# An engine order left to the scheduler, four tiles for spilled sums, and the start of MLP 2, in an attention kernel with two MLPs

## The chip, the core and the metric

The kernel runs on one core of a Trainium2 chip. The metric is the device time of one execution, in microseconds (us). The core has five engines, each with a queue of its own that it works off in order: TensorE (PE; matmuls, weight loads as PEld), VectorE (DVE), ScalarE (ACT), GpSimd (POOL) and SyncE (SP), which issues all transfers (DMAs) here. An instruction waits until what it needs is there, and everything behind it on its engine waits with it. Results of matmuls stand in PSUM, of which the program uses eight banks (four of each of two tags, a and b); the other memory on the core is SBUF.

## The reference, cut to what matters

Attention of 8 heads (4 batches, 512 local positions with a window of 32 to each side, 32 global ones), then an MLP with a gate (MLP 1), then an MLP with a rational function (MLP 2), on 2176 tokens of 512 numbers.

```python
def _moe_ref(x, w_gate, w_val, w_out):            # 512 -> 1536 -> 512
    g = x @ w_gate
    silu = g * (1.0 / (1.0 + np.exp(-g)))
    val = x @ w_val
    return (silu * val @ w_out).astype(np.float32)

def _moe2_ref(x, w_in, w_out, a, b):              # 512 -> 2048 -> 512
    h = x @ w_in
    h2 = h * h
    h3 = h2 * h
    P = a[0] + a[1] * h + a[2] * h2 + a[3] * h3
    Q = 1.0 + np.abs(b[0]) * np.abs(h) + np.abs(b[1]) * h2
    g = P / (Q + 1e-06)
    return (g @ w_out).astype(np.float32)

def reference(**kwargs):
    attn_out = _attn_ref(**attn_kwargs)
    B, H, S, D = attn_out.shape
    x = np.ascontiguousarray(attn_out.transpose(0, 2, 1, 3)).reshape(B * S, H * D)
    x = _moe_ref(x=x, **moe_kwargs)
    return _moe2_ref(x=x, **moe2_kwargs)
```

## The kernel before

Every matmul of the MLPs is done in three: both operands are split into a high part (a cast, ScalarE or VectorE, L126 or L128) and a low part (a subtraction, GpSimd or VectorE, L129), and `mm3` (L485 to L487) adds high x high, high x low and low x high. The weights come as 64-bit floats; each block of 512 columns is loaded as 32-bit halves into one of two tiles `stage` (L134) and converted by GpSimd (L144), ScalarE (L146) and VectorE (L147, L149).

The first part (to about 277 us) is the attention with a third of MLP 1's hidden layer woven in. Its partial sums of MLP 1 go to a tensor `yas` in HBM.

The second part is the rest of MLP 1. It runs in eight passes `v`: batch `v % 4`, first with hidden blocks 4 to 7 (v = 0 to 3), then with blocks 8 to 11 (v = 4 to 7). A pass has four units `u`, one for each hidden block. A unit makes gate and value by a scheme with seven products of half blocks in place of eight: seven `prod` of six matmuls each, into the PSUM banks X and Z (tag b) and Y (tag a). Three copies on ScalarE take intermediate sums out of PSUM: L769 (of X), L773 (of Z) and L776 (of X again, before TensorE adds the last product to X). Between L773 and L776 stands the Silu (L754) of the unit before, which waits for an addition of VectorE (L753). TensorE goes on with X after L776, so a late L776 holds TensorE. The operands of these products are x and differences of its halves (`x_prep`, parts 0 to 7: differences on VectorE, L721, high parts on ScalarE, low parts on VectorE).

The products with the output weights of a pass are made in the next pass, in eight *pieces* (`piece`), two or three to a unit (in v = 1 four in units 1 and 2). For v < 4, VectorE adds a piece to the partial sum fetched from `yas` (L806) into one of two tiles "y" (L814), and it is stored back (L815). For v = 4 to 7, a whole block is fetched into `x32` (L822), and the pieces are added there (L818): that is MLP 2's input. Meanwhile MLP 2's weights are converted, one block in units 0 and 1 and two in units 2 and 3, and stored in a tensor `w2s` (L860). In the last pass they are fetched back (L871) and split (`w2_item`).

The third part is MLP 2, in tiles of 384 tokens by one of 16 hidden blocks: `p2_mm`, then ScalarE (L1038 to L1040, L1067, L1068, L1073) and VectorE (L1047 to L1059), then the low part (L1062, on GpSimd for the first four tiles) and `p2_out` (L1086 to L1088), four tiles behind.

The order of TensorE and SyncE is that in which the code is written, everywhere. For VectorE, ScalarE and GpSimd a scheduler sets the order when the kernel is built, by a cost model of its own, except inside `tc.manual_schedule()`: there it is the written order too. The kernel before enters this ahead of the second part (`ordered[0].__enter__()`) and leaves it ahead of `p2_mm(0)`.

Of the kernel before, what the change touches and what calls it, by code (L numbers as in the profile page):

```python
# [77 lines left out]
def tile_attn_moe_moe(  # L78
# [575 lines left out]
    for name, n, count in (("ab", HT, 2), ("v2", HT, 2), ("s", 2 * HT, 2), ("t", 2 * HT, 3), ("y", HT, 2),  # L654
                           ("e", 256, 1), ("st", 512, 2)):
        FA[name] = [("f", at_ + n * i, n) for i in range(count)]
        at_ += n * count
# [55 lines left out]
    def x_prep(v, part):  # L713
        b = v % B
        t0 = b * S
        b11, b12 = x32[:, 0:2, t0:t0 + HT], x32[:, 0:2, t0 + HT:t0 + S]
        b21, b22 = x32[:, 2:4, t0:t0 + HT], x32[:, 2:4, t0 + HT:t0 + S]

        def diff(which, p, q):
            t = tv[v, which] = take["t"]().rearrange("p (k c) -> p k c", k=2)  # L720
            nc.vector.tensor_tensor(out=t, in0=p, in1=q, op=ALU.subtract)  # L721
            return t
        if part == 0:
            x_split(v, B11, b11)
        elif part == 1:
            x_split(v, T1, diff(T1, b12, b11))
        elif part == 2:
            x_split(v, T2, diff(T2, b22, tv[v, T1]))
        elif part == 3:
            diff(T4, b21, tv[v, T2])  # L730
            diff(T3, b22, b12)
        elif part == 4:
            x_split(v, B21, b21)
        elif part == 5:
            x_split(v, T3, tv[v, T3])
        elif part == 6:
            x_split(v, B22, b22)
        else:
            x_split(v, T4, tv[v, T4])
# [68 lines left out]
    def piece_evac(v, i):  # L808
# [3 lines left out]
        if v < B:  # L812
            y = py.pop((v, i))
            nc.vector.tensor_tensor(out=y, in0=o, in1=y, op=ALU.add)  # L814
            nc.sync.dma_start(yas[:, j, t0:t0 + HT], y)  # L815
        else:
            x = x32[:, j, t0:t0 + HT]
            nc.vector.tensor_tensor(out=x, in0=o, in1=x, op=ALU.add)  # L818

# [77 lines left out]
    ordered = [tc.manual_schedule()]  # L897
    ordered[0].__enter__()
# [27 lines left out]
    first_pieces = {1: (0, 4), 2: (4, 8)}  # L926
    for v in range(NV):
        fs = FB[v // B]
        for u, f in enumerate(fs):
# [16 lines left out]
            def before():  # L946
                todo(words[0])
                if (v, u) == (4, 2):
                    todo("")
# [6 lines left out]
            def after():  # L956
                n0, n1 = (first_pieces if v == 1 else pieces_of).get(u, (0, 0)) if v else (0, 0)
                if v and v - 1 < B:
                    for i in range(n0, min(n0 + 2, n1)):
                        piece_load(v - 1, i)  # L960
# [3 lines left out]
                for i in range(n0, n1):  # L964
                    piece(v - 1, i, FB[(v - 1) // B], True, True)
                    if v - 1 < B and i + 2 < n1:
                        piece_load(v - 1, i + 2)
# [11 lines left out]
                if v >= B and u == 0:  # L979
# [13 lines left out]
    for k in range(KD):  # L993
        split_y(0, k)
    for i in range(4):
        piece(v, i, fs[:3], True, False)
    for i in range(4):
        piece(v, i, fs[3:], False, True)
    for i in range(4, 8):
        piece(v, i, fs, True, True)  # L1000
    w2_item(24, nc.vector, nc.gpsimd)

    total = NC2 * F2
    ph, pt, pq, pr, pg = {}, {}, {}, {}, {}

    def width(n):
        c = n // F2
        return cols2[c][1] - cols2[c][0]

    def p2_mm(n):  # L1010
        c, f = divmod(n, F2)
        w = width(n)
        h = psum("b")
        for k in range(KD):
            mm3(h[:, :w], wt2[f, 0], slice(128 * k, 128 * k + 128), xs[("y", c), k], slice(0, w),
                k == 0, k == KD - 1)
        ph[n] = h[:, :w]

    warm_act = const.tile([128, 1], F32, name="warm_act")
    nc.scalar.activation(warm_act, cqt, AF.Abs_reciprocal_sqrt)  # L1020
    ordered.pop().__exit__(None, None, None)
    p2_mm(0)
    p2_mm(1)

# [79 lines left out]
    for n in range(total + 4):  # L1104
# [21 lines left out]
        if n < 8:  # L1126
            w2_item(24 + n + 1, nc.vector, nc.gpsimd)
# [62 lines left out]
```

## Time and profile before

| what | us |
|---|---|
| median of 3 runs (lowest, highest) | 1080.92 (1076.33, 1082.48) |
| the profiled execution, its own time | 1079.84 |
| its span, first to last instruction | 1078.1 |
| TensorE busy | 944.5 (88%) |
| VectorE busy | 775.4 (72%) |
| ScalarE busy | 620.5 (58%) |
| GpSimd busy | 228.7 (21%) |

The mean granted clock of TensorE is 0.935 of full speed. Busy times are sums over the whole span, and a busy TensorE may be one at half its clock. "Idle before" is the time that an engine stood still ahead of an instruction, with the instruction or transfer that ended it. A wait for several things is put down to the last.

### The profile page before, as it was taken

To read this page: it belongs to the slowest core of one execution; us is meant where nothing else is said; L and a number is where in the kernel's file an instruction comes from. 1 tells how busy PE (TensorE), PEld (TensorE's weight loads), DVE (VectorE), ACT (ScalarE), POOL (GpSimd) and SP (SyncE) were. 2 spreads that over 40 slices of the span, in tenths; PEclk is the share of its full clock that TensorE was granted. 3 is DMA by queue.
4 is the path that set the end of the run, shared out by engine and by line. 5 is a ranking of instruction groups with operands and counts; after the bars stand their busy time and mean duration, and the time that the engine had idled before them with its cause. 6 is when DMAs were issued, how large, how long until landed. Compare 5 with 4: busy or idle time off the path is not lost.

```text
span 1078.1 us, 20901 instructions
## 1 busy us (share of the span) xinstructions
PE 944.5 (88%) x7986; PEld 865.5 (80%) x7988; DVE 775.4 (72%) x1740; ACT 620.5 (58%) x1450; POOL 228.7 (21%) x233
## 2 busy tenths in 40 slices
PE   6989999999676787767678999779999999999998
PEld 4778888889676677666677999669999999999996
DVE  5876667667354555465567755999888988888897
ACT  5755566544353233334244343557877878878786
POOL 2420000002433222335142235840000000000012
PEclk8889999999778888978789999889999999999999
DMA  9846878634113344435353332310100101001010
GB/s 341 294 143 232 279 226 277 194 116 126 61 40 113 130 140 135 146 112 200 115 186 124 105 130 79 118 40 1 30 1 1 30 1 30 1 1 30 1 30 21
DMA packets 62981, 118.02 MB, mean 109 GB/s; under 512 B 8352, under 2 KB 31904, under 8 KB 62880
## 3 DMA queue, kind: packets, MB, share of 16 engines
q1 hardware_dynamic: 62880, 116.68, 32.7%
q8 instruction: 63, 1.03, 0.4%
q14 instruction: 38, 0.31, 0.1%
HBM read 88.61 MB, written 28.05 MB: 108 GB/s over the span
## 4 chain that ended last, share of the span: by engine, by line
PE 42%; DMA 20%; DVE 15%; issue 10%; POOL 6%; ACT 5%; SPq 1%; POOLq 0%; DVEq 0%; ACTq 0%
PE b L485 7%; PE b L487 7%; PE b L486 7%; DMA stage<-in_w_dram 7%; PE a L1088 5%; PE a L1087 5%; PE a L1086 5%; DMA w2s<-stage 4%; DMA arf<-yas 2%; POOL stage L144 2%; DVE stage L147 2%; POOL arr L129 2%; ACT e L313 2%; DMA arf<-w1s 2%; DMA yas<-arf 2%
## 5 line engine op out<-in xcount | busy, mean ns | idle before, releaser
L129 POOL TENSOR_TENSOR arr<-arf,arr 128x256 fp32r<-128x256 f32 (+2 forms) x66 | 74.0, 1134 | 204.3 <-ACT arr L126 183.1
L485 PE MATMUL b<-arl,arr 128*128 128x272 f32 x176 | 57.7, 328 | 55.4 <-ACT arf L776 43.9
L1038 ACT ACTIVATE arf<-b,cst 128x384 f32<-128x384 f32 (+1 forms) x96 | 62.8, 654 | 70.1 <-PE b L487 69.6
L144 POOL TENSOR_SCALAR stage<-stage 128x512 f32<-128x512 f32 x68 | 54.0, 798 | 203.9 <-DMA stage<-in_w_dram 157.3
L485 PE MATMUL b<-arl 128*128 128x272 f32 x208 | 66.5, 320 | 30.0 <-ACT arf L776 17.3
L147 DVE SCALAR_TENSOR_TENSOR stage<-stage 128x512 int32<-128x512 int32 x68 | 49.4, 727 | 55.4 <-POOL stage L144 49.8
L1062 POOL TENSOR_TENSOR arr<-arf,arr 128x256 fp32r<-128x256 f32 (+1 forms) x19 | 16.5, 868 | 340.5 <-ACT arr L1073 340.5
L485 PEld LDWEIGHTS b<-arl,arr 128*128 128x128 f32 x176 | 37.5, 213 | 59.2 <-ACT arf L776 47.1
L485 PE MATMUL b<-xy,wa 128*128 128x256 f32 (+1 forms) x256 | 79.4, 310 | 4.5 <-DVE mn L307 2.2
L486 PE MATMUL a<-arr 128*128 128x272 f32 x256 | 77.6, 303 | 3.0 <-POOL arr L129 3.0
L1052 DVE TENSOR_TENSOR arf<-arf,b 128x384 f32<-128x384 f32 (+1 forms) x96 | 51.0, 531 | 38.6 <-ACT arf L1039 38.3
L485 PE MATMUL a<-arr 128*128 128x272 f32 x256 | 77.3, 302 | 0.1
L487 PE MATMUL b<-xy,wa 128*128 128x256 f32 (+1 forms) x256 | 75.9, 296 | 1.5 <-POOL wa L129 1.5
L487 PE MATMUL a<-arr 128*128 128x272 f32 x256 | 76.8, 300 | 0.0
L486 PE MATMUL b<-xy,wa 128*128 128x256 f32 (+1 forms) x256 | 75.3, 294 | 0.4 <-DVE xy L129 0.4
L146 ACT ACTIVATE stage<-stage 128x512 int32<-128x512 uint32 x68 | 45.6, 681 | 51.5 <-DMA stage<-in_w_dram 40.8
L1088 PE MATMUL a<-arl,arr 128*128 128x512 f32 x170 | 67.7, 398 | 5.7 <-POOL arr L1062 3.0
L485 PEld LDWEIGHTS b<-arl 128*128 128x128 f32 x208 | 43.6, 210 | 32.8 <-ACT arf L776 19.2
L1048 DVE SCALAR_TENSOR_TENSOR arf<-arf,cst 128x384 f32<-128x384 f32 (+1 forms) x96 | 69.7, 726 | 0.0
L1086 PE MATMUL a<-arl,arr 128*128 128x512 f32 x170 | 67.1, 394 | 1.8 <-ACT arr L1073 1.8
L1040 ACT ACTIVATE arf<-arf,cst 128x384 f32<-128x384 f32 (+1 forms) x96 | 66.5, 693 | 3.1
L1087 PE MATMUL a<-arl,arr 128*128 128x512 f32 x170 | 67.6, 398 | 0.0
(172 smaller groups left out, 3359.7 us busy)
## 6 DMA issues: line engine op xcount, KB each, us to landing
stage<-in_w_dram SPq DMA_DIRECT2D x68, 512.0 KB, 4.3
v<-in_vw_dram SPq DMA_DIRECT2D x16, 512.0 KB, 6.5
w2s<-stage SPq DMA_DIRECT2D x32, 256.0 KB, 2.5
stage<-w2s SPq DMA_DIRECT2D x16, 512.0 KB, 3.5
v<-in_vw_dram SPq DMA_DIRECT2D x16, 384.0 KB, 4.9
w1s<-stage SPq DMA_DIRECT2D x24, 256.0 KB, 2.4
arf<-w1s SPq DMA_DIRECT2D x24, 256.0 KB, 3.1
arf<-yas SPq DMA_DIRECT2D x32, 136.0 KB, 3.9
```

The lines of the kernel that those rows point to most:

```text
L129: eng_lo.tensor_tensor(out=lo, in0=src, in1=hi.bitcast(F32), op=ALU.subtract)
L144: nc.gpsimd.tensor_scalar(out=high.bitcast(F32), in0=high.bitcast(F32), scalar1=2.0 ** -112, scalar2=1.0, op0=ALU.mult, op1=ALU.mult)
L147: nc.vector.scalar_tensor_tensor(out=low, in0=high, scalar=3, in1=low, op0=ALU.logical_shift_left, op1=ALU.bitwise_or)
L485: nc.tensor.matmul(o, w[:, 0, wsl], x[:, 0, xsl], start=first, stop=False, skip_group_check=go_on)
L486: nc.tensor.matmul(o, w[:, 0, wsl], x[:, 1, xsl], start=False, stop=False, skip_group_check=go_on)
L487: nc.tensor.matmul(o, w[:, 1, wsl], x[:, 0, xsl], start=False, stop=last, skip_group_check=go_on)
L1038: nc.scalar.activation(pt[n], h, AF.Identity, bias=NA2, scale=NA3)
L1040: nc.scalar.activation(pq[n], a, AF.Identity, bias=B0, scale=B1)
L1048: nc.vector.scalar_tensor_tensor(out=t2, in0=t2, scalar=NA0, in1=r2, op0=ALU.add, op1=ALU.mult)
L1086: nc.tensor.matmul(o, g[:, 0, gsl], w[:, 0], start=(f == 0), stop=False)
L1087: nc.tensor.matmul(o, g[:, 0, gsl], w[:, 1], start=False, stop=False)
L1088: nc.tensor.matmul(o, g[:, 1, gsl], w[:, 0], start=False, stop=(f == F2 - 1))
```

## The change

The second part is no longer inside `manual_schedule()`, so the scheduler orders VectorE, ScalarE and GpSimd there as well (TensorE and SyncE keep the written order). The room of one tile "t" becomes two more tiles "y": there are four. T2 and T4 are now made in place in T1's tile. The fetch of partial sums is issued up to four pieces ahead, from unit 3 of the pass before on, and the store of a unit's pieces in the next unit. The fetch of the block for v = 4 moves from unit 0 to unit 3. In front of the last four pieces of the last pass stand the first two tiles of MLP 2 (`p2_mm(0)`, `p2_mm(1)`), and the last 20 splits of MLP 2's weights are made with ScalarE in place of VectorE.

```diff
--- before.py
+++ after.py
@@ -651,7 +651,7 @@
-    for name, n, count in (("ab", HT, 2), ("v2", HT, 2), ("s", 2 * HT, 2), ("t", 2 * HT, 3), ("y", HT, 2),
+    for name, n, count in (("ab", HT, 2), ("v2", HT, 2), ("s", 2 * HT, 2), ("t", 2 * HT, 2), ("y", HT, 4),
                            ("e", 256, 1), ("st", 512, 2)):
@@ -725,9 +725,12 @@
         elif part == 2:
-            x_split(v, T2, diff(T2, b22, tv[v, T1]))
+            t2 = tv[v, T1]
+            nc.vector.tensor_tensor(out=t2, in0=b22, in1=t2, op=ALU.subtract)
+            x_split(v, T2, t2)
         elif part == 3:
-            diff(T4, b21, tv[v, T2])
+            t4 = tv[v, T4] = tv[v, T1]
+            nc.vector.tensor_tensor(out=t4, in0=b21, in1=t4, op=ALU.subtract)
             diff(T3, b22, b12)
@@ -810,12 +813,16 @@
         if v < B:
-            y = py.pop((v, i))
+            y = py[v, i]
             nc.vector.tensor_tensor(out=y, in0=o, in1=y, op=ALU.add)
-            nc.sync.dma_start(yas[:, j, t0:t0 + HT], y)
...
+    def piece_store(v, i):
+        j, half = divmod(i, 2)
+        t0 = (v % B) * S + HT * half
+        nc.sync.dma_start(yas[:, j, t0:t0 + HT], py.pop((v, i)))
...
@@ -894,8 +901,23 @@
-    ordered = [tc.manual_schedule()]
-    ordered[0].__enter__()
...
+    ordered = []
...
             def before():
                 todo(words[0])
-                if (v, u) == (4, 2):
-                    todo("")
+                if 0 < v <= B:
+                    n0, n1 = plan_of(v).get(u, (0, 0))
+                    m0, m1 = plan_of(v).get(u - 1, (0, 0))
+                    for i in range(m0, m1):
+                        piece_store(v - 1, i)
+                    while loaded[0] < min(8, m1 + 4):
+                        piece_load(v - 1, loaded[0])
+                        loaded[0] += 1
...
             def after():
-                n0, n1 = (first_pieces if v == 1 else pieces_of).get(u, (0, 0)) if v else (0, 0)
-                if v and v - 1 < B:
-                    for i in range(n0, min(n0 + 2, n1)):
-                        piece_load(v - 1, i)
+                n0, n1 = plan_of(v).get(u, (0, 0)) if v else (0, 0)
                 todo(words[2])
...
                 for i in range(n0, n1):
                     piece(v - 1, i, FB[(v - 1) // B], True, True)
-                    if v - 1 < B and i + 2 < n1:
-                        piece_load(v - 1, i + 2)
...
-                if v >= B and u == 0:
+                if u == 3:
+                    loaded[0] = 0
+                    if v < B:
+                        for i in range(4):
+                            piece_load(v, i)
+                        loaded[0] = 4
+                if v >= B and u == (3 if v == B else 0):
                     load_ya(v)
...
@@ -992,35 +1026,18 @@
     for k in range(KD):
         split_y(0, k)
+    w2_item(14, nc.scalar, nc.gpsimd)
     for i in range(4):
         piece(v, i, fs[:3], True, False)
     for i in range(4):
         piece(v, i, fs[3:], False, True)
+    warm_act = const.tile([128, 1], F32, name="warm_act")
+    nc.scalar.activation(warm_act, cqt, AF.Abs_reciprocal_sqrt)
+    p2_mm(0)
+    p2_mm(1)
     for i in range(4, 8):
         piece(v, i, fs, True, True)
-    w2_item(24, nc.vector, nc.gpsimd)
+    w2_item(24, nc.scalar, nc.gpsimd)
...
-    warm_act = const.tile([128, 1], F32, name="warm_act")
-    nc.scalar.activation(warm_act, cqt, AF.Abs_reciprocal_sqrt)
-    ordered.pop().__exit__(None, None, None)
-    p2_mm(0)
-    p2_mm(1)
...
         if n < 8:
-            w2_item(24 + n + 1, nc.vector, nc.gpsimd)
+            w2_item(24 + n + 1, nc.scalar, nc.gpsimd)
```


SyncE, from the fetch of the last weights ahead of v = 1 on; `yas` holds the partial sums, `arf` the tiles "y" (and others), `w1s` and `w2s` converted weights. Before:

```order
L673 DMA arf<-w1s 128x512 x8
L806 DMA arf<-yas 128x272 x2
L134 DMA stage<-in_w_dram 128x1024
L815 DMA yas<-arf 128x272
L806 DMA arf<-yas 128x272
L815 DMA yas<-arf 128x272
L806 DMA arf<-yas 128x272
L815 DMA yas<-arf 128x272 x2
L860 DMA w2s<-stage 128x512
L134 DMA stage<-in_w_dram 128x1024 x2
```

The same place in the changed kernel (L806, L815 and L860 are L809, L825 and L867 there):

```order
L673 DMA arf<-w1s 128x512 x6
L809 DMA arf<-yas 128x272 x4
L673 DMA arf<-w1s 128x512 x2
L134 DMA stage<-in_w_dram 128x1024
L867 DMA w2s<-stage 128x512
L134 DMA stage<-in_w_dram 128x1024 x2
L825 DMA yas<-arf 128x272 x4
L809 DMA arf<-yas 128x272 x4
L867 DMA w2s<-stage 128x512
L134 DMA stage<-in_w_dram 128x1024
```

Before, fetches and stores of single tiles alternate; now four fetches stand ahead of the first conversion, the four stores in one row behind two loads of weights, and four fetches right after them.

ScalarE, unit 2 of pass v = 1, from its first copy to the first copy of the next unit; `arl<-arf` 128x544 is a part of x, `arr<-arf` 128x544 the hidden layer, `stage` a conversion. Before:

```order
L769 COPY arf<-b 128x272
L126 CAST arl<-arf 128x544
L773 COPY arf<-b 128x272
L754 ACTIVATE arf<-arf 128x544
L776 COPY arf<-b 128x272
L126 CAST arr<-arf 128x544
L126 CAST arl<-arf 128x544
L146 ACTIVATE stage<-stage 128x512 x2
L769 COPY arf<-b 128x272
```

The same in the changed kernel (the copies L769, L773, L776 are L772, L776, L779, the Silu L757):

```order
L772 COPY arf<-b 128x272
L146 ACTIVATE stage<-stage 128x512
L776 COPY arf<-b 128x272
L146 ACTIVATE stage<-stage 128x512
L757 ACTIVATE arf<-arf 128x544
L779 COPY arf<-b 128x272
L126 CAST arr<-arf 128x544
L146 ACTIVATE stage<-stage 128x512
L772 COPY arf<-b 128x272
```

Two of the conversions have moved in between the three copies, and the parts of x have left this unit.

ScalarE, from the last hidden layer of MLP 1 to the first reciprocal square root of MLP 2; `x_82` is x32. Before:

```order
L126 CAST arr<-arf 128x544
L126 CAST arr<-x_82 128x384 x4
L1020 ACT_TABLE_LOAD
L1020 ACTIVATE warm_act<-cqt 128x1
L1038 ACTIVATE arf<-b,cst 128x384
L1039 ACTIVATE arf<-b 128x384
L1040 ACTIVATE arf<-arf,cst 128x384
L1038 ACTIVATE arf<-b,cst 128x384
L1039 ACTIVATE arf<-b 128x384
L1067 ACTIVATE arf<-arf,cqt 128x384
```

In the changed kernel (L1038 to L1040 are L1055 to L1057, L1067 is L1084):

```order
L126 CAST arr<-arf 128x544
L126 CAST arl<-stage 128x512 x4
L1055 ACTIVATE arf<-b,cst 128x384
L1056 ACTIVATE arf<-b 128x384
L1057 ACTIVATE arf<-arf,cst 128x384
L126 CAST arl<-stage 128x512 x2
L1055 ACTIVATE arf<-b,cst 128x384
L126 CAST arl<-stage 128x512 x2
L1084 ACT_TABLE_LOAD
L1084 ACTIVATE arf<-arf,cqt 128x384
L1056 ACTIVATE arf<-b 128x384
L1085 ACTIVATE arf<-arf 128x384
```

The splits of x32 have moved ahead of the hidden layer, the splits of weights (from `stage`) stand among the first tiles' instructions, and the table is loaded ahead of the first L1084.

## Rows read from the trace of the kernel before

**Rows 1.** The page's head: span and instructions.

```profile
span 1078.1 us, 20901 instructions
```

**Rows 2.** Stretches: us, busy of each engine, PEclk (granted clock), DMA, GB/s.

```profile
277.30:318.70 41.40, 29.16 (x176) 28.08 (x175) 17.17 (x32) 18.20 (x41) 16.99 (x19) 0.75 0.20 62
318.70:375.80 57.10, 39.87 (x277) 38.82 (x275) 30.73 (x53) 19.05 (x39) 14.46 (x14) 0.86 0.35 114
375.80:428.40 52.60, 40.08 (x264) 38.88 (x264) 29.11 (x53) 17.53 (x37) 11.70 (x13) 0.85 0.40 133
428.40:486.70 58.30, 40.56 (x264) 39.36 (x264) 33.03 (x56) 20.05 (x45) 18.91 (x21) 0.82 0.42 139
486.70:547.80 61.10, 41.28 (x264) 39.87 (x264) 34.98 (x60) 22.73 (x52) 23.89 (x27) 0.83 0.48 158
547.80:589.50 41.70, 35.32 (x264) 34.33 (x264) 30.55 (x51) 17.01 (x35) 12.51 (x11) 0.96 0.43 141
589.50:623.70 34.20, 33.20 (x249) 32.66 (x250) 25.03 (x46) 15.17 (x32) 8.34 (x7) 0.95 0.32 111
...
688.20:722.00 33.80, 24.77 (x94) 19.93 (x95) 33.80 (x47) 18.15 (x35) 22.41 (x16) 0.85 0.22 74
```

**Rows 3.** TensorE's waits, 318.7 to 547.8 us: us, times, longest.

```profile
PE b L485 <- ACT arf L776: 51.2, 13, 9.8
PE b L485 <- ACT arf L769: 10.6, 3, 4.5
```

**Rows 4.** TensorE's waits, 547.8 to 623.7 us.

```profile
PE b L485 <- ACT arf L769: 9.1, 2, 5.0
```

**Rows 5.** VectorE's timeline, 337 to 349 us: start, duration, instruction, [idle before].

```profile
342.24 0.44 DVE L814 TENSOR_TENSOR arf<-a,arf 128x272 f32<-128x272 f32 x1 [3.63 <-DMA arf<-yas]
345.10 0.44 DVE L814 TENSOR_TENSOR arf<-a,arf 128x272 f32<-128x272 f32 x1 [2.42 <-DMA arf<-yas]
```

**Rows 6.** ScalarE's timeline, 335 to 350 us.

```profile
346.20 0.65 ACT L126 CAST arl<-arf 128x544 fp32r<-128x544 f32 x1 [8.70 <-DVE arf L721]
...
348.62 0.37 ACT L776 COPY arf<-b 128x272 f32<-128x272 f32 x1
```

**Rows 7.** SyncE's timeline, 337 to 348 us.

```profile
338.29 0.32 SPq L815 DMA_DIRECT2D yas<-arf  x1
340.02 0.32 SPq L806 DMA_DIRECT2D arf<-yas  x1
```

**Rows 8.** L814: what ended VectorE's idle time before it, us, times.

```profile
  DMA arf<-yas: 35.4, 12
```

**Rows 9.** The fetches L806: issue to landing.

```profile
DMA to landing us min/median/max: 2.1/3.9/7.8
```

**Rows 10.** ScalarE's waits, 258 to 700 us.

```profile
ACT stage L146 <- DMA stage<-in_w_dram: 24.8, 9, 4.0
```

**Rows 11.** VectorE's groups, 688.2 to 722 us (last row 722 to 1068).

```profile
L1048 DVE SCALAR_TENSOR_TENSOR arf<-arf,cst 128x384 f32<-128x384 f32 x6 | 9.6, 1595 | 0.0
L128 DVE CAST arr<-stage 128x512 fp32r<-128x512 f32 x8 | 4.4, 561 | 0.0
L128 DVE CAST arl<-stage 128x512 fp32r<-128x512 f32 x4 | 3.2, 845 | 0.0
...
L1048 DVE SCALAR_TENSOR_TENSOR arf<-arf,cst 128x384 f32<-128x384 f32 x74 | 46.5, 629 | 0.0
```

**Rows 12.** TensorE's waits, 664 to 722 us.

```profile
PE a L1086 <- ACT arr L1073: 7.9, 3, 5.7
PE a L1088 <- POOL arr L1062: 4.4, 3, 3.0
```

**Rows 13.** GpSimd's groups, 655 to 722 us.

```profile
L129 POOL TENSOR_TENSOR arl<-stage,arl 128x512 fp32r<-128x512 f32 x15 | 21.6, 1462 | 3.3 <-DVE arl L128 1.7 <-ACT arl L126 1.6
```

**Rows 14.** ScalarE's timeline, 660 to 664 us.

```profile
662.37 1.28 ACT L1020 ACT_TABLE_LOAD   x1
```

**Rows 15.** The stores L860: issue to landing.

```profile
DMA to landing us min/median/max: 2.0/2.5/4.6
```

More of the change, by code (lines that the diff above doesn't have):

```diff
@@ L895, in split_y, with width, p2_mm @@
         xs[("y", c), k] = t
-    ordered = [tc.manual_schedule()]
-    ordered[0].__enter__()
+    total = NC2 * F2
+    ph, pt, pq, pr, pg = {}, {}, {}, {}, {}
+    def width(n):
+        c = n // F2
+        return cols2[c][1] - cols2[c][0]
+    def p2_mm(n):
+        c, f = divmod(n, F2)
+        w = width(n)
+        h = psum("b")
+        for k in range(KD):
+            mm3(h[:, :w], wt2[f, 0], slice(128 * k, 128 * k + 128), xs[("y", c), k], slice(0, w),
+                k == 0, k == KD - 1)
+        ph[n] = h[:, :w]
+    ordered = []
     def a_end():
@@ L926, in tile_attn_moe_moe, with plan_of @@
     first_pieces = {1: (0, 4), 2: (4, 8)}
+    loaded = [0]
+    def plan_of(v):
+        return first_pieces if v == 1 else pieces_of
     for v in range(NV):
@@ L998, in tile_attn_moe_moe @@
         piece(v, i, fs[3:], False, True)
+    warm_act = const.tile([128, 1], F32, name="warm_act")
+    nc.scalar.activation(warm_act, cqt, AF.Abs_reciprocal_sqrt)
+    p2_mm(0)
+    p2_mm(1)
     for i in range(4, 8):
         piece(v, i, fs, True, True)
-    w2_item(24, nc.vector, nc.gpsimd)
[L1003 to L1017, printed above, removed]
-    warm_act = const.tile([128, 1], F32, name="warm_act")
-    nc.scalar.activation(warm_act, cqt, AF.Abs_reciprocal_sqrt)
-    ordered.pop().__exit__(None, None, None)
-    p2_mm(0)
-    p2_mm(1)
+    w2_item(24, nc.scalar, nc.gpsimd)
     NA0, NA1, NA2, NA3, B0, B1 = (cst[:, i:i + 1] for i in range(6))
```

## The prediction

> **What bounds the kernel now.** I read the busy time by stretches first, one stretch for each pass v of the second part, cut at the first ScalarE copy (L769) of the pass [rows 1, 2]. The reader is to see that the four passes v = 1 to 4, which spill and fetch partial sums, take 57.1, 52.6, 58.3 and 61.1 us (229.1 us), while v = 5 and v = 6, with the same matmuls, the same preparation of x and the same conversion of weights but no fetched sums, take 41.7 and 34.2 us. In v = 6 TensorE is busy for 33.20 of 34.20 us, so 34.2 us is about what the matmuls of a pass cost. In v = 1 to 4 no engine is full: VectorE, the busiest besides TensorE, has 30.73, 29.11, 33.03 and 34.98 us, 127.85 us together. These passes are bound by waits.
>
> The waits of TensorE in v = 1 to 4 are almost all one kind: 51.2 us in 13 waits for the copy L776, 10.6 us in 3 for L769 [rows 3]; in v = 5 and 6 the wait for L769 stays, with 9.1 us in 2 [rows 4]. The copy itself takes 0.37 us, so something ahead of it in ScalarE's queue is late. In v = 1, u = 2, that is seen: VectorE stops at L814, the addition of the fetched sum, for 3.63 us and then 2.42 us, each time for the transfer arf<-yas, [rows 5], and only then makes the difference L721. ScalarE's split of that difference has waited 8.70 us, and L773, L754 and L776 stand behind it [rows 6]. The transfer is late because there are two tiles: SyncE stores one at 338.29, and fetches the next into it only at 340.02, when the store has landed [rows 7]. Over the kernel VectorE stands 35.4 us in 12 such waits [rows 8].
>
> TensorE's time off is paid for twice. The excess of v = 1 to 4 over four times 34.2 us is 229.1 - 136.8 = 92.3 us, but the waits are 51.2 + 10.6 = 61.8 us. The granted clock is 0.82 to 0.86 in those passes and 0.95 in v = 6 [rows 2]: after each stop matmuls run at the lower level for a while. So 1 us of wait goes with 92.3 / 61.8 = 1.49 us of time.
>
> The second place is the start of MLP 2, 664.0 to 722.0 us. TensorE waits 7.9 us for the first results of ScalarE (L1073), 4.4 us for GpSimd's halves [rows 12], and from 688.2 to 722.0 VectorE has no idle time at all, 33.80 of 33.80 us [rows 2].
>
> **The change part by part.** *Four tiles for spilled sums, fetched a unit ahead, stored a unit later.* The two SyncE excerpts show it: in place of store, fetch, store, fetch there are four fetches, then stores of four, then four fetches. A fetch lands 3.9 us (median, 7.8 at most) after its issue [rows 9]; now a unit, 9 us or more by the clean passes, lies between, so L814 should wait for no transfer. How much comes back, I take from v = 5, which is the same pass without fetches: there VectorE is idle for 41.70 - 30.55 = 11.15 us. Give v = 1 to 4 their own VectorE work and this idle time: 127.85 + 4 x 11.15 = 172.5 us, or 56.6 us less. That leaves the conversions' waits in. The bounds: half of it (28 us), if half of the fetches are still late behind SyncE's other waits; 92.3 us, if all four passes become as short as v = 6. I take 56.6, since v = 5 has as much VectorE work as they have. What is late next is the conversion: ScalarE waits 24.8 us in 9 waits, up to 4.0 us, for its weights [rows 10].
>
> The two differences that are now made in place (T2 over T1, T4 over T2) free the room for the two tiles. Each must wait until its tile has been split; the work is unchanged, VectorE has other work to put there, and I cost it at nothing; without that cover it is a wait of some 0.7 us, as before the low halves, twice a pass, 10 us over seven passes. The fetch of whole blocks (L822) moves back three units for v = 4; its readers, the additions L818 of v = 5, stand a unit later in VectorE's order. Nothing for that either.
>
> *The scheduler's order in the second part.* TensorE's order does not change there. ScalarE's does, as the excerpt of v = 1, u = 2 shows: conversions (L146) that stood behind the high half of a unit now stand between the copies. I count 13 of the 32 between the first and third copy of their unit, none before. An L146 whose weights have landed costs 0.68 us of ScalarE there; one that has not holds the copies, and TensorE behind them. This is not to be had from the trace of before. Bound on the side of loss: 13 waits of 4.0 us, the longest seen [rows 10], at 1.49 is 77 us. Bound on the side of gain: v = 5 falls to 34.2 us (7.5), and v = 0, which takes 41.4 us at a clock of 0.75 [rows 2] because seven splits of weights stand in a row ahead of a copy, gives 10. I take 0: the conversions are spread more evenly (one for half a unit instead of two in a row ahead of L769), which helps the waits for L769, and the small delays between Silu and L776 eat that.
>
> *Two tiles of MLP 2 ahead of the last four pieces, and 20 splits of W2 on ScalarE instead of VectorE.* On VectorE these are 20 casts; from 688.2 to 722.0 us 12 of them take 4.4 + 3.2 = 7.6 us [rows 11]. VectorE is the bound there, so they count in full. The tiles come 48 matmuls earlier, 6 us at the pace of v = 6, which could take the whole first wait for L1073, 5.7 us. But in ScalarE's new order twelve casts stand between the last hidden layer and the first L1073, and GpSimd's twelve low halves, 1.46 us each [rows 13], need 17.5 us; begun at 664, they leave the first result complete at 682 us at the earliest, and later by what they wait for transfers. I take 3 us of the 5.7. The activation table, 1.28 us, was loaded in idle time (L1020) [rows 14]; its dummy activation has moved to the start of the kernel, where it is of no use, and the load now stands ahead of the first L1067. That is 1 us lost. Sum: 7.6 + 3 - 1, some 10 us; bounds 0 and 16.
>
> VectorE's additions of two SBUF tiles take 1595 ns (L1048) while GpSimd makes its halves and 629 ns afterwards [rows 11]. The Trainium skill (SBUF — State Buffer, Who interferes with whom) says that a VectorE instruction with two SBUF inputs and a GpSimd instruction that reads SBUF exclude each other. By that rule GpSimd's 20 halves, which the change keeps, go on holding VectorE up; the trace agrees with these two durations.
>
> **The sum.** 56.6 + 0 + 10 = 66.6 us. The profiled execution took 1079.84 us (span 1078.1 and 1.7 around it), 1.1 us under the median of the three runs, 1080.92. 1079.84 - 66.6 = 1013.2. I say 1013.
>
> **The rivals.**
> 1. *All of the waits go.* Fetches and conversions are both hidden: 92.3 (v = 1 to 4) + 7.5 (v = 5) + 10 (MLP 2) = 110, 970 us. For it: the conversions are spread out, and SyncE no longer stands before a fetch. Against it: VectorE's 34.98 us in v = 4 leave nothing for its waits inside a unit. Chance of 960 to 1000: 0.25.
> 2. *GpSimd holds VectorE.* Its halves now come packed from 664 us on, just under the first tiles; L1048 stays at 1.6 us for these, the first result is as late as before (688.2), and the start of MLP 2 gives 0: 1023 us. For it: 1595 against 629 ns [rows 11], and the rule above. Against it: 7.6 us of casts leave a full engine. Chance 0.10.
> 3. *The order gives part back.* The 13 conversions ahead of a third copy wait 2 us each on average: 13 x 2 x 1.49 = 39, 1052 us. For it: ScalarE is in order, and a wait there reaches TensorE within a matmul group. Chance of 1030 to 1070: 0.13.
> 4. *It is slower.* The same place, but each such conversion comes right after the store that frees its tile, and waits for the whole way round: a store lands after 2.5 us [rows 15], a load takes up to 4.0 us of waiting, 6.5 us together; 13 x 6.5 x 1.49 = 126, so 1139 us. It decides from a mean wait of (66.6 + 5.4) / (13 x 1.49) = 3.7 us on. Against it: the mean wait of before is 24.8 / 9 = 2.8 us, and 23 of 32 conversions waited for nothing. Chance 0.07.
> 5. *Nothing comes of it*: the additions L814 wait for TensorE instead of the fetch, and the passes are bound elsewhere. v = 5 speaks against it. Within 0.5%: 0.03.
>
> **How the numbers follow.** The forecast, 1000 to 1030, has 0.42, and with rivals 1 to 5 that makes 1. A range from 975 to 1050 leaves out the lower part of rival 1, the upper of 3, and 4 and 5, some 0.2 together. 0.5% (5.4 us) is about what can be told from no change. Faster 0.42 + 0.25 + 0.10 + 0.13 = 0.90, same 0.03, slower 0.07.
>
> **What would show it.** L814 waits for arf<-yas less than 5 us in all. v = 1 to 4 take 38 to 46 us each, with the granted clock over 0.9; v = 5 to 7 stay within 3 us. What is left of TensorE's waits goes back to L146 waiting for its transfer. From 688 to 722 us VectorE has no L128 cast and has idle time; ScalarE loads a table just ahead of the first L1067. Wrong would be: passes of over 50 us without waits of L814, which means that the new order costs what the fetches gave, or waits of L814 as before.

## The result, and the profile after

The changed kernel takes 1004.14 us (median of 4 runs, 1002.59 to 1005.75) against 1080.92 before: a ratio of 0.9298, 95% interval 0.926 to 0.9337, so 7.0% less. A fourth execution of the kernel before took 2213.38 us and is not counted. The profiled execution spans 1002.3 us (before: [rows 1]) at a granted clock of 0.964 (0.935).

The stretches of the changed kernel, cut like [rows 2] at the first copy of each pass (L769 is L772 now), v = 0 to 6, and the start of MLP 2; columns as there:

```profile
281.30:313.00 31.70, 26.29 (x171) 25.53 (x172) 16.57 (x32) 17.47 (x41) 14.78 (x17) 0.84 0.17 52
313.00:357.80 44.80, 37.10 (x261) 36.22 (x260) 31.45 (x52) 19.35 (x43) 21.82 (x20) 0.89 0.51 156
357.80:396.90 39.10, 36.27 (x280) 35.04 (x278) 28.00 (x50) 16.30 (x34) 8.78 (x10) 1.00 0.58 177
396.90:434.90 38.00, 32.84 (x254) 31.90 (x254) 32.54 (x55) 19.20 (x42) 17.49 (x19) 1.00 0.56 175
434.90:477.70 42.80, 36.54 (x271) 35.23 (x270) 34.61 (x57) 22.00 (x51) 26.00 (x27) 0.96 0.64 200
477.70:521.40 43.70, 36.48 (x259) 35.32 (x258) 31.22 (x55) 17.79 (x36) 12.70 (x13) 0.88 0.57 182
521.40:559.10 37.70, 35.27 (x265) 34.61 (x264) 25.54 (x49) 15.37 (x31) 9.65 (x9) 0.95 0.34 113
...
612.00:646.00 34.00, 29.46 (x145) 26.11 (x144) 26.68 (x41) 26.92 (x53) 20.20 (x16) 0.90 0.21 63
```

v = 1 to 4 take 164.7 us, 64.4 less than the 229.1 of before, and v = 0 is 9.7 shorter. v = 5 and 6 are longer (81.5 against 75.9, +5.6). The rest of the difference of 75.8 us between the spans: +4.0 ahead of the second part, +0.8 in the first three units of v = 7, and -12.0 from the last first copy to the end.

TensorE's waits in v = 1 to 4 of the changed kernel (L779 is the copy L776 of [rows 3]; us, times, longest):

```profile
PE b L485 <- ACT arf L779: 17.4, 10, 5.3
PE a L486 <- POOL arr L129: 3.7, 3, 1.4
PE b L485 <- ACT arf L772: 0.8, 2, 0.4
```

They were 51.2 and 10.6 us; 21.9 are left in all. ScalarE's waits in the same stretch:

```profile
ACT stage L146 <- DMA stage<-in_w_dram: 24.3, 13, 6.8
ACT arf L772 <- PE b L487: 19.5, 7, 5.8
ACT arf L757 <- DVE arf L756: 12.0, 9, 2.7
```

The conversion that waits for its weights is now first; next, ScalarE stands at L772 waiting for TensorE, so it is ahead of it there. What ended VectorE's idle time before the additions L817 (L814 before, [rows 8]):

```profile
  PE a L487: 8.8, 8
```

No addition waits for a transfer any more, where 35.4 us went.

VectorE's L1065 at the start of MLP 2 in the changed kernel, 612 to 646 us, and then 646 to 1002 (busy, mean ns; L1065 is L1048 of [rows 11]):

```profile
L1065 DVE SCALAR_TENSOR_TENSOR arf<-arf,cst 128x384 f32<-128x384 f32 x6 | 5.4, 906 | 0.0
...
L1065 DVE SCALAR_TENSOR_TENSOR arf<-arf,cst 128x384 f32<-128x384 f32 x74 | 45.1, 609 | 0.0
```

The casts L128 are gone, and VectorE is busy for 26.68 of 34.00 us, no longer for all of them. ScalarE's timeline there:

```profile
612.79 1.15 ACT L126 CAST arl<-stage 128x512 fp32r<-128x512 f32 x2 [0.64 <-DMA stage<-w2s]
613.96 1.28 ACT L1084 ACT_TABLE_LOAD   x1
615.25 0.62 ACT L1084 ACTIVATE arf<-arf,cqt 128x384 f32<-128x384 f32 x1
```

The table is loaded ahead of the first L1084, at the same 1.28 us as in [rows 14].

### The profile page after: what moved, and what is told of

Its sections match the earlier page's. It is cut to its first block, busy times and chain, and to the rows that moved or that the text cites. A ratio compares the mean times of both kernels' runs of the same rounds, so it can differ in the third digit from the quotient of the medians.

```text
span 1002.3 us, 20914 instructions
## 1 busy us (share of the span) xinstructions
PE 924.2 (92%) x7988; PEld 847.2 (85%) x7988; DVE 759.0 (76%) x1720; ACT 627.9 (63%) x1471; POOL 230.3 (23%) x233
## 3 DMA queue, kind: packets, MB, share of 16 engines
q1 hardware_dynamic: 62880, 116.68, 35.9%
## 4 chain that ended last, share of the span: by engine, by line
PE 52%; DMA 18%; DVE 11%; POOL 6%; ACT 6%; issue 4%; SPq 2%; POOLq 0%; ACTq 0%; DVEq 0%
DMA stage<-in_w_dram 10%; PE b L485 9%; PE b L487 8%; PE b L486 8%; PE a L1105 6%; PE a L1104 6%; PE a L1103 6%; PE a L486 3%; PE a L487 3%; PE a L485 3%; POOL arr L129 3%; DMA w2s<-stage 2%; DVE stage L147 2%; ACT e L313 2%; DVE stage L149 2%
## 5 line engine op out<-in xcount | busy, mean ns | idle before, releaser
L144 POOL TENSOR_SCALAR stage<-stage 128x512 f32<-128x512 f32 x68 | 48.7, 718 | 251.7 <-DMA stage<-in_w_dram 203.4
L129 POOL TENSOR_TENSOR arr<-arf,arr 128x544 fp32r<-128x544 f32 (+2 forms) x66 | 81.6, 1254 | 100.0 <-ACT arr L126 94.0
L1055 ACT ACTIVATE arf<-b,cst 128x384 f32<-128x384 f32 (+1 forms) x96 | 62.7, 653 | 56.1 <-PE b L487 55.5
L147 DVE SCALAR_TENSOR_TENSOR stage<-stage 128x512 int32<-128x512 int32 x68 | 54.5, 803 | 49.9 <-POOL stage L144 45.9
L146 ACT ACTIVATE stage<-stage 128x512 int32<-128x512 uint32 x68 | 46.0, 678 | 60.2 <-DMA stage<-in_w_dram 49.7
L486 PE MATMUL a<-arr 128*128 128x272 f32 x256 | 76.5, 299 | 6.7 <-POOL arr L129 6.7
L485 PE MATMUL a<-arr 128*128 128x272 f32 x256 | 76.3, 298 | 4.7 <-ACT arr L126 4.7
L487 PE MATMUL a<-arr 128*128 128x272 f32 x256 | 76.1, 297 | 1.1 <-POOL arr L129 1.1
L485 PE MATMUL b<-arl 128*128 128x272 f32 x208 | 63.3, 304 | 14.9 <-ACT arf L779 10.1
L485 PE MATMUL b<-arl,arr 128*128 128x272 f32 x176 | 54.2, 308 | 16.1 <-ACT arf L779 15.9
L1057 ACT ACTIVATE arf<-arf,cst 128x384 f32<-128x384 f32 (+1 forms) x96 | 66.3, 690 | 3.3 <-ACT arf L1056 0.4
L1103 PE MATMUL a<-arl,arr 128*128 128x512 f32 x170 | 66.5, 391 | 0.0
L1065 DVE SCALAR_TENSOR_TENSOR arf<-arf,cst 128x384 f32<-128x384 f32 (+1 forms) x96 | 64.0, 667 | 0.0
L485 PE MATMUL b<-arr,arl 128*128 128x384 f32 (+1 forms) x192 | 63.2, 329 | 0.0
L486 PE MATMUL b<-arr,arl 128*128 128x384 f32 (+1 forms) x192 | 63.2, 329 | 0.0
```

Source lines behind the costliest of these rows:

```text
L129: eng_lo.tensor_tensor(out=lo, in0=src, in1=hi.bitcast(F32), op=ALU.subtract)
L147: nc.vector.scalar_tensor_tensor(out=low, in0=high, scalar=3, in1=low, op0=ALU.logical_shift_left, op1=ALU.bitwise_or)
L485: nc.tensor.matmul(o, w[:, 0, wsl], x[:, 0, xsl], start=first, stop=False, skip_group_check=go_on)
L486: nc.tensor.matmul(o, w[:, 0, wsl], x[:, 1, xsl], start=False, stop=False, skip_group_check=go_on)
L487: nc.tensor.matmul(o, w[:, 1, wsl], x[:, 0, xsl], start=False, stop=last, skip_group_check=go_on)
L1055: nc.scalar.activation(pt[n], h, AF.Identity, bias=NA2, scale=NA3)
```

## The experiments

The trace alone says that the waits went, not which part of the change took them. Theory F is the prediction's own accounting: the tiles bring some 56 us, the order nothing, the start of MLP 2 some 10. Its rival S says that the scheduler's order carries a large part and the tiles less. The table has the runs that are compared pass by pass, by the starts of first copies in the traces: time of the four units of v = 1 to 4 in pairs, of v = 5 and of v = 6. For scale, v = 6 of before is 19.0 + 15.2 us, four times which is 76.0 and 60.8.

| kernel | us (median) | v = 1-4, units 0, 1 | units 2, 3 | v = 5 | v = 6 |
|---|---|---|---|---|---|
| before | 1080.92 | 83.8 | 145.3 | 41.7 | 34.2 |
| tiles alone (e1) | 1047.90 | 85.6 | 104.5 | 48.5 | 34.3 |
| tiles, fetched just ahead (e11) | 1050.48 | 83.7 | 113.3 | 41.7 | 34.3 |
| order alone (e2) | 1064.03 | 126.3 | 74.2 | 57.9 | 35.7 |
| all but the order (e4) | 1038.49 | 86.2 | 103.9 | 47.9 | 34.4 |
| all, ScalarE as written (e6) | 1019.93 | 88.3 | 95.0 | 40.3 | 32.9 |
| all, VectorE as written (e7) | 1043.57 | 105.9 | 85.1 | 47.4 | 44.1 |
| the change | 1004.14 | 89.8 | 74.9 | 43.8 | 37.7 |
| the change, no conversions (e12) | 980.26 | 85.1 | 66.5 | 35.9 | 34.2 |

**The parts apart.** e1 is the kernel before with the tiles (T2 and T4 in place with them), the early fetch, the late store and the block for v = 4 fetched in unit 3; the second part stays in the written order.

```diff
-    for name, n, count in (("ab", HT, 2), ("v2", HT, 2), ("s", 2 * HT, 2), ("t", 2 * HT, 3), ("y", HT, 2),
+    for name, n, count in (("ab", HT, 2), ("v2", HT, 2), ("s", 2 * HT, 2), ("t", 2 * HT, 2), ("y", HT, 4),
...
+                    for i in range(m0, m1):
+                        piece_store(v - 1, i)
+                    while loaded[0] < min(8, m1 + 4):
+                        piece_load(v - 1, loaded[0])
+                        loaded[0] += 1
```

> Of the change only the four tiles, the early fetches and the late stores; the second part stays in the written order and the start of MLP 2 as before. Theory F (the fetches were the wait): passes v = 1 to 4 fall from 229 us to 165 to 175 us together, L814 (now the addition in piece_evac) waits for no transfer, the time is 1018 to 1028 us, ratio 0.94 to 0.95. Theory S (the scheduler's order fills the waits, whatever they are for): the stretch stays above 200 us and the time above 1050 us, because ScalarE and VectorE still stand in a row behind each conversion.

Measured 1047.90 us, 0.9691 (0.9647 to 0.9735) of before: between the two theories. v = 1 to 4 fall by 39.0 us, to 190.1, and v = 5 rises by 6.8. TensorE's waits in e1, 320 to 540 us:

```profile
PE b L485 <- ACT arf L779: 24.9, 14, 4.0
PE b L485 <- ACT arf L772: 17.7, 4, 7.2
```

and two of VectorE's:

```profile
DVE x L820 <- DMA x<-yas: 6.2, 1, 6.2
DVE arf L817 <- DMA arf<-yas: 2.3, 2, 1.4
```

The additions hardly wait for a transfer, yet the copies are still late. The four waits for L772 stand at the starts of v = 2 to 5. In the written order the second conversion of the last unit is ahead of that copy on ScalarE, and it has waited 3.7 to 4.4 us for its weights.

e2 is the kernel before without the written order, nothing else.

```diff
-    ordered = [tc.manual_schedule()]
-    ordered[0].__enter__()
+    ordered = []
...
-    ordered.pop().__exit__(None, None, None)
```

> Of the change only the scheduler's order in the second part; two tiles for spilled sums, stored and fetched in turn as before, the start of MLP 2 as before. F: store and fetch still alternate on SyncE and VectorE's additions still wait for them, so v = 1 to 4 stay above 215 us; v = 0 falls by 10 us as in the whole change; the time is 1060 to 1080 us. S: v = 1 to 4 fall below 190 us and the time is under 1040 us.

Measured 1064.03 us, 0.9856 (0.9812 to 0.99). The time is what F had room for, but v = 1 to 4 at 200.5 are not. The order takes units 2 and 3 from 145.3 to 74.2 us, as far as the whole change does, and gives 42.5 back in units 0 and 1, and 16.2 in v = 5. TensorE's waits in e2, 320 to 540 us:

```profile
PE a L485 <- DVE arf L814: 36.0, 6, 13.2
PE b L485 <- ACT arf L776: 11.7, 7, 2.7
```

A piece's PSUM bank is not free until its addition is made. The longest wait, on SyncE, VectorE and TensorE, and SyncE's own longest waits, 320 to 540 us:

```profile
487.71 0.90 SPq L806 DMA_DIRECT2D arf<-yas  x2
492.13 0.44 DVE L814 TENSOR_TENSOR arf<-a,arf 128x272 f32<-128x272 f32 x1 [1.84 <-DMA arf<-yas]
492.62 0.59 PE L485 MATMUL a<-arr 128*128 128x272 f32 x1 [13.24 <-DVE arf L814]
...
SPq L134 <- DMA w2s<-stage: 49.2, 21, 4.2
```

The addition is late because its fetch is. SyncE, in the written order, issues the fetch at 487.71, behind four stores and four loads of conversions that it began at 469.48 and that the faster units 2 and 3 have left over; each load waits for the store that frees its tile. The wait of 13.0 us in v = 3 looks the same. In the change the fetches stand ahead of these transfers. No run has the scheduler's order with four tiles and late fetches, so it isn't shown whether the tiles alone would do.

e3 is the kernel before with MLP 2's first two tiles ahead of the last four pieces and the splits on ScalarE; e4 is the whole change with the second part in the written order again.

```diff
+    w2_item(14, nc.scalar, nc.gpsimd)
...
+    p2_mm(0)
+    p2_mm(1)
     for i in range(4, 8):
         piece(v, i, fs, True, True)
-    w2_item(24, nc.vector, nc.gpsimd)
+    w2_item(24, nc.scalar, nc.gpsimd)
```

> Of the change only the start of MLP 2: two tiles ahead of the last four pieces and 20 splits on ScalarE, all in the written order. If the split's engine and the tiles' place are what counts: 10 to 12 us less, 1069 to 1072 us. If the 12 us of the whole change come from the scheduler's order of these instructions: within 4 us of before, since ScalarE's casts then stand in one block ahead of the first tile.

```diff
-    ordered = []
+    ordered = [tc.manual_schedule()]
+    ordered[0].__enter__()
```

> The whole change, but the second part (to the last split ahead of MLP 2) in the written order. F: the scheduler's order is worth little either way, 1000 to 1015 us; its gain in v = 0 (10 us) is missing, its loss in v = 5 and 6 (6 us) too. S: above 1035 us.

e3: 1072.82 us, 0.993 (0.9902 to 0.9959); from the last first copy to the end it is 8.6 us shorter. e4: 1038.49 us, 0.9602 (0.956 to 0.9645), where F was wrong and S right. Tiles and start add up without the order (32.1 and 7.2 alone, 41.5 together, against 1080.03 in the same session); the order on top of them brings 1038.49 - 1004.14 = 34 us.

**Which engine's order.** e6 is the whole change with ScalarE alone in the written order in the second part, e7 with VectorE alone (TensorE and SyncE are in it everywhere).

```diff
-    ordered = []
+    ordered = [tc.manual_schedule(engines={mybir.EngineType.PE, mybir.EngineType.SP, mybir.EngineType.Activation})]
+    ordered[0].__enter__()
```

> The whole change, but ScalarE's instructions of the second part in the written order; VectorE and GpSimd stay with the scheduler. The whole change is 34 us faster than with all three engines in the written order (1004 against 1038). Theory A: the gain is ScalarE's, where L146, splits and copies share one queue and a copy that is late holds TensorE at once; then this kernel is near 1038, above 1025. Theory V: the gain is VectorE's (a conversion or a difference ahead of L753 holds the Silu); then it is below 1015.

> The whole change, but VectorE's instructions of the second part in the written order; ScalarE and GpSimd stay with the scheduler. Theory A: near 1004, below 1015. Theory V: above 1025. If both this one and the one with ScalarE in written order are above 1025, the gain needs the two orders together.

e6: 1019.93 us, 0.9426 (0.9376 to 0.9476); e7, with `DVE` in place of `Activation`: 1043.57 us, 0.9638 (0.9587 to 0.969). Theory A falls: ScalarE's new order without VectorE's brings nothing over e4's 0.9602. VectorE's without ScalarE's brings half of the 34 us (0.9602 to 0.9426), and ScalarE's on top of it the rest (to 0.9298); so V's bound of 1015 us is missed too. GpSimd is with the scheduler in both runs, and its part is not told apart. In v = 1 to 4 neither order does much alone: 190.0 us in e4, 183.3 in e6, 191.0 in e7, but 164.7 with both. TensorE's waits for the copies in these passes and up to the first copy of v = 5, two lines each of e4 (319.6 to 509.6 us), e6 (312.6 to 495.9) and e7 (317.4 to 508.4):

```profile
PE b L485 <- ACT arf L779: 22.1, 14, 3.9
PE b L485 <- ACT arf L772: 18.8, 5, 7.1
...
PE b L485 <- ACT arf L772: 18.3, 4, 6.0
PE b L485 <- ACT arf L779: 16.1, 7, 5.2
...
PE b L485 <- ACT arf L779: 40.0, 12, 8.2
PE b L485 <- ACT arf L772: 0.2, 1, 0.2
```

In the change they are 17.4 and 0.8. The waits for L772, behind the conversions, go with ScalarE's order. But with VectorE in the written order the waits for L779 then grow to 40.0; with VectorE's order as well they are 17.4.

Both waits are seen in unit 3 of v = 3. VectorE's timeline in e1:

```profile
440.00 1.04 DVE L733 TENSOR_TENSOR arf<-x,arf 128x544 f32<-128x544 f32 x1
440.96 1.16 DVE L721 TENSOR_TENSOR arf<-x 128x544 f32<-128x544 f32 x1
442.04 0.68 DVE L147 SCALAR_TENSOR_TENSOR stage<-stage 128x512 int32<-128x512 int32 x1
...
443.37 1.13 DVE L817 TENSOR_TENSOR arf<-a,arf 128x272 f32<-128x272 f32 x3
444.41 0.68 DVE L147 SCALAR_TENSOR_TENSOR stage<-stage 128x512 int32<-128x512 int32 x1
...
445.74 0.42 DVE L701 TENSOR_TENSOR arf<-arf 128x256 f32<-128x256 f32 x1
446.07 0.43 DVE L756 TENSOR_TENSOR arf<-b,arf 128x272 f32<-128x272 f32 x1
```

and ScalarE's, in the same kernel:

```profile
440.42 0.39 ACT L772 COPY arf<-b 128x272 f32<-128x272 f32 x1 [0.53 <-PE b L487]
446.19 0.71 ACT L126 CAST arl<-arf 128x256 fp32r<-128x256 f32 x2 [5.38 <-DVE arf L701]
446.81 0.38 ACT L776 COPY arf<-b 128x272 f32<-128x272 f32 x1
...
447.64 0.37 ACT L779 COPY arf<-b 128x272 f32<-128x272 f32 x1
...
454.72 0.67 ACT L146 ACTIVATE stage<-stage 128x512 int32<-128x512 uint32 x1 [3.73 <-DMA stage<-in_w_dram]
```

VectorE waits for no transfer here. The work left over from unit 2 (differences of x, two conversions, three additions) stands ahead of L701, a difference of weights. ScalarE's split of that waits 5.38 us and the three instructions behind it with it; TensorE stands 3.92 us for L779. At the unit's end a conversion that has waited 3.73 us for its weights holds the next first copy, and TensorE stands 1.48 us for that. The unit takes 14.9 us. VectorE in the changed kernel at the same place:

```profile
425.13 1.24 DVE L701 TENSOR_TENSOR arf<-arf 128x256 f32<-128x256 f32 x1
...
426.65 0.42 DVE L817 TENSOR_TENSOR arf<-a,arf 128x272 f32<-128x272 f32 x1
428.32 0.69 DVE L147 SCALAR_TENSOR_TENSOR stage<-stage 128x512 int32<-128x512 int32 x1 [1.25 <-POOL stage L144]
...
429.66 0.78 DVE L817 TENSOR_TENSOR arf<-a,arf 128x272 f32<-128x272 f32 x2
...
430.99 0.43 DVE L756 TENSOR_TENSOR arf<-b,arf 128x272 f32<-128x272 f32 x1
```

L701 is ahead of the additions, the conversion is one and not two, and between L772 (428.90) and the next (434.93) lie 6.0 us. But the late L701 is not the whole cause. In e7 it comes as late after the unit's first copy as in e4 (3.5 and 3.8 us), and the unit takes 7.8 us against 13.0: ScalarE there makes the copy L776 ahead of the split of L701, and no conversion waits ahead of the next first copy.

**Number of tiles, or how early.** e11 is e1 with the fetches just ahead of their unit's pieces, each store at once, and the block for v = 4 in unit 0 again, as before; only the number of tiles (and with it the in-place differences) is left.

```diff
             nc.vector.tensor_tensor(out=y, in0=o, in1=y, op=ALU.add)
+            piece_store(v, i)
...
+                if v and v - 1 < B:
+                    for i in range(n0, n1):
+                        piece_load(v - 1, i)
...
-                if v >= B and u == (3 if v == B else 0):
+                if v >= B and u == 0:
```

> The tiles alone, written order: four tiles, but each unit fetches its pieces just ahead of them and stores each at once, as before the change, and the block for v = 4 is fetched in unit 0. Theory N (two tiles made store and fetch take turns): most of the 39 us in v = 1 to 4 stays, 195 to 205 us, and v = 5 is back at 42 us; 1045 to 1053 us. Theory P (the fetch must be a unit ahead): the additions wait 2 to 4 us in each of 12 units, v = 1 to 4 at 210 to 225 us, 1062 to 1078 us.

1050.48 us, 0.9724 (0.969 to 0.9759): v = 1 to 4 at 197.0, as theory N had it, so 32.1 of the 39.0 us come from the number; the additions wait 1.6 us in all for transfers. Fetching a unit ahead and storing a unit later add 6.9, which e1 pays back in v = 5: there VectorE stands 6.2 us for the block (L820, above), and in e11 v = 5 is at the 41.7 of before.

**The moved block by itself.** e5 is the change with that fetch in unit 0 again.

```diff
-                if v >= B and u == (3 if v == B else 0):
+                if v >= B and u == 0:
```

> The whole change, with the fetch of the block for v = 4 (L822, L829 in the change) back in unit 0. In the run with the tiles alone VectorE waited 6.2 us for this fetch at the start of v = 5, where I had costed the move at nothing. If the move costs: v = 5 falls by 2 to 6 us and the time is 998 to 1002 us. If the scheduler's order already hides it (its additions stand a unit later): 1002 to 1006 us, or up to 1010 us if the block and the fetched sums are in each other's way in v = 4.

1009.94 us, 0.9345 (0.93 to 0.939); v = 5 is 46.3, not shorter. With the scheduler's order the later fetch costs nothing.

**What is left.** e12 is the change without the conversion of MLP 2's weights (no loads, conversions or stores of them); the last pass fetches numbers of another tensor in their place.

```diff
-            nc.sync.dma_start(st, w2s[f])
+            nc.sync.dma_start(st, kT[f % B].rearrange("p a b -> p (a b)")[:, 0:1024])
...
-                    conv.begin()
+                    pass
```

> The whole change without the conversion of MLP 2's weights: the loads, the three engines' instructions on them and the stores are left out, and the last pass takes other numbers of the same size from HBM as weights, so MLP 2's result is another. This measures what conversions still cost in v = 1 to 6. If what is left of TensorE's waits is L146 and its transfers: v = 1 to 4 fall from 164.7 to 140 to 150 us, v = 5 and 6 from 81.5 to 68 to 72 us, 970 to 985 us. If VectorE's own work (differences, low halves, sums, 30 to 35 us in a pass) holds them: v = 1 to 4 stay above 155 us.

980.26 us, 0.9069 (0.9036 to 0.9101): v = 1 to 4 at 151.6, 13.1 less than the change, and v = 5 and 6 at 70.1, 11.4 less. The conversions still cost some 24 us. Without them v = 5 and 6 stand 1.7 us above twice 34.2, v = 1 to 4 still 14.8 above four times that, between the two expectations. It doesn't say which of the load, the three engines' work and the store costs how much.

e8 tries the wait that v = 5 begins with (4.5 us for a split, L126): the last output weights are fetched earlier. Its three pieces in unit 2 of v = 4 read weights of block 9 in place of block 4's.

```diff
-        (4, 2): ("w,11,3 l,9,2 l,10,2", "", ""),
-        (4, 3): ("", "", "o,9 o,10 l,11,2"),
+        (4, 2): ("w,11,3 l,9,2 l,10,2", "", "o,9"),
+        (4, 3): ("l,11,2", "", "o,10"),
```

> The whole change, with the last output weights (block 11) fetched ahead of unit 3 of v = 4 in place of behind it, and the split of block 9 a unit earlier for that. TensorE waits 4.5 us at the start of v = 5 for a split of output weights on ScalarE (arr L126), in a unit of 17.3 us. If this fetch is what is late: that wait goes, v = 5 falls by 4 to 8 us, 996 to 1001 us. If the split is late because the scheduler has put it behind two conversions: the wait stays, 1002 to 1006 us.

1004.74 us, 0.9298 (0.9248 to 0.9347): v = 5 falls to 38.1, and v = 4 rises to 49.0, where the pieces of unit 2 now wait 3.2 us for the split of block 9. They read it only because it has taken block 4's place, so the run doesn't show whether the wait could go.

e9 takes ScalarE back into the written order from v = 5 on, where e6 was shorter than the change.

```diff
+        if v == 5:
+            ordered.append(tc.manual_schedule(engines={mybir.EngineType.PE, mybir.EngineType.SP, mybir.EngineType.Activation}))
+            ordered[0].__enter__()
...
     unit_finish()()
+    ordered.pop().__exit__(None, None, None)
```

> The whole change, with ScalarE back in the written order from pass v = 5 to the end of the second part, VectorE and GpSimd left to the scheduler. In the run with ScalarE in written order throughout, v = 5 and 6 took 73.2 us against 81.5 in the whole change, and v = 7 0.8 us less. If ScalarE's early conversions are what those passes lose by: 8 to 9 us less, 993 to 998 us. If the 73.2 us depended on what v = 1 to 4 had left behind: 1000 to 1005 us.

1008.37 us, 0.9341 (0.9303 to 0.938), a miss: v = 5 and 6 take 79.7 us, not e6's 73.2, and the end 419.7 against 412.3; why the end is longer is open. No version run here with the whole computation beats the change.

**The splits' engine.** e10 is the change with 18 of the last 20 splits on VectorE again; the two that now stand ahead of the pieces (`w2_item(14, ...)`) stay on ScalarE.

```diff
-    w2_item(24, nc.scalar, nc.gpsimd)
+    w2_item(24, nc.vector, nc.gpsimd)
...
-            w2_item(24 + n + 1, nc.scalar, nc.gpsimd)
+            w2_item(24 + n + 1, nc.vector, nc.gpsimd)
```

> The whole change, with the last splits of MLP 2's weights on VectorE again (the two tiles stay ahead of the last pieces). My sum gave the engine 7.6 us of the 10 at the start of MLP 2: 1010 to 1013 us, and the stretch from the last first copy to the end 419 to 421 us in place of 412.3. If the place of the two tiles and the order are what counts: 1002 to 1006 us.

1009.53 us, 0.935 (0.9312 to 0.9388): 5.4 us by the medians, with intervals that overlap. The trace has it at the place: v = 7 is 3.2 longer and the stretch to the end 2.7.

## Why the prediction was right, and where its sum was off

The direction and the sum held: 66.6 us forecast, 75.8 between the spans, 1013 against 1004. Two terms were wrong in opposite directions: the tiles were put 24.5 us over what they bring alone (32.1 in e1), the order 34 under what it brings on top. That the sum came within 9.2 us is in part luck.

- **Four tiles, 56.6 us: mis-sized.** The mechanism is shown, since L817 waits for no transfer in the change, and e11 gives 32.1 us in v = 1 to 4 by the number of tiles. But alone the tiles bring 39.0 in v = 1 to 4. I had given these passes v = 5's idle time of VectorE, 11.15 us each. In e1 they have 190.1 us less VectorE's busy 30.48, 30.89, 32.59 and 36.88, that is 59.3 of idle time or 14.8 each, and 3.0 us more work. The leftover lies in units 2 and 3 (104.5 against 60.8), where two conversions a unit and, in v = 3 and 4, the differences of weights stand in the written order ahead of what the next copy needs. v = 5 itself has such a wait, 12.4 us in its unit 3 against 5.4 in v = 6. I had read the late copy as the fetch's fault alone [rows 5, 6], but the fetch was only the first of the things that were late.
- **The scheduler's order, 0: mis-sized, and the larger mistake.** It brings 16 us alone and 34 with the rest; in v = 1 to 4, 190.0 to 164.7, and in v = 0, 40.6 to 31.7 (e4 to the change), though v = 0 begins 2.8 later. The working had one part of the gain, conversions no longer in a row ahead of the first copy, and let small delays eat it: TensorE's waits for that copy fall from 18.8 us in e4 to 0.8. It did not have the other, which of VectorE's work stands ahead of a copy. In v = 1 to 4 neither does much alone (e6, e7). The order also needs the tiles, or the early fetches that they allow: with fetches behind the conversions on SyncE, as before, it loses 42.5 us in units 0 and 1 (e2).
- **The loss that I set against it is real, and smaller than the gain.** Two conversions between copies hold TensorE in unit 2 of v = 1. ScalarE's timeline of the changed kernel:

```profile
336.37 0.66 ACT L146 ACTIVATE stage<-stage 128x512 int32<-128x512 uint32 x1 [3.20 <-DMA stage<-in_w_dram]
336.93 0.37 ACT L776 COPY arf<-b 128x272 f32<-128x272 f32 x1
339.92 0.65 ACT L146 ACTIVATE stage<-stage 128x512 int32<-128x512 uint32 x1 [2.62 <-DMA stage<-in_w_dram]
...
341.02 0.37 ACT L779 COPY arf<-b 128x272 f32<-128x272 f32 x1
```

  and TensorE's, behind them:

```profile
341.44 0.60 PE L485 MATMUL b<-arl,arr 128*128 128x272 f32 x1 [5.25 <-ACT arf L779]
```

  That unit takes 18.6 us, against 11.7 in e1 and 11.3 without conversions (e12). This is rival 3's and 4's mechanism. It doesn't decide: ScalarE waits 24.3 us for weights in these passes, and TensorE only 17.4 us for L779, whatever made it late; 8.2 us of that kind are left without conversions (e12). In v = 5 and 6 ScalarE's order costs 8.3 us (81.5 against e6's 73.2), but e9 doesn't get them back.
- **The moved block L822, nothing.** Wrong for the written order (6.8 us in e1's v = 5), right for the scheduler's (e5).
- **v = 6 as a clean pass, 34.2 us.** The working gives it the same conversions as the others. The trace has three L146 in it and six in each of v = 2 to 5. The 34.2 us hold all the same: with no conversion at all v = 6 takes 34.2 and v = 2 34.4 (e12).
- **T2 and T4 in place, nothing.** No run has this apart from the tiles whose room it makes.
- **The start of MLP 2, 10 us.** 12.0 from the last first copy on in the change, 8.6 in e3. Of it the engine of the splits, 7.6 in the working, is worth some 5 (e10, for 18 of the 20).
- **1.49 us for 1 us of wait** was the price at many waits. In the change v = 1 to 4 exceed 136.8 by 27.9 us at 21.9 of waits, 1.27.

Of what was to show it: the passes are within 38 to 46 us; the clock is over 0.9 in three of the four (0.89 in v = 1); v = 5 and 7 are within 3 us, v = 6 is 3.5 over; and ScalarE's longest wait is the conversions'. Rival 1 is what e12 does by leaving them out. Rival 2's mechanism is there: L1065 takes 906 ns beside GpSimd's halves and 609 afterwards. The Trainium skill's rule (SBUF — State Buffer, Who interferes with whom), that two SBUF inputs on VectorE and a GpSimd read exclude each other, agrees with these durations. But 906 is far under the 1595 of before, and VectorE now has idle time. What GpSimd's halves still cost there is not shown: no run takes them away.

## What to carry to other kernels

A stage without the suspected transfer is a fair measure of what its removal brings only if nothing else is queued ahead of the critical instruction: list all that stands ahead of that instruction on each in-order engine, not only what waited longest. Buffers and order are worth more together than apart (32.1 + 7.2 + 16.0 us alone, 76.8 together), and an order that lets TensorE run ahead gives its gain back where the transfers that it needs next stand behind others in SyncE's queue (e2). The orders of two engines can need each other in the same way (e6, e7). Where a move shortens one pass, look at the passes beside it: the earlier fetch gains 6.9 us in v = 1 to 4 of e1 and gives 6.8 back in v = 5.

## What the runs showed of the hardware that was not expected

Passes with waits left in them can run at the full granted clock: v = 2 and 3 are at 1.00 (2.4 GHz) with TensorE busy for 36.27 of 39.10 and 32.84 of 38.00 us, where before all four were at 0.82 to 0.86. In v = 1, with the wait of 5.25 us, it is 0.89. The load of the activation table costs no more than its 1.28 us: the activation behind it starts 0.01 us after its end.
